# A range test of the softmax sums, and a general path behind a branch, in a fused attention and max-out kernel

## The chip, the core and the metric

The kernel runs on one core of a Trainium2 chip. The engines are TensorE (PE: matmul, with its weight loads shown apart as PEld), VectorE (DVE), ScalarE (ACT), GpSimd (POOL) and SyncE (SP), which here only issues DMA transfers. Each engine runs its own stream of instructions in order, and they wait for one another through semaphores. The metric is the device time of one execution in microseconds, lower is better.

## What is computed

Attention over queries that are averaged in pairs, followed by a two-branch max-out layer on the result:

```python
def _attn_ref(q, k, v):                       # q, k, v: (8, 8, 1152, 64)
    q_pool = q.reshape(B, H, S // 2, 2, D).mean(axis=3)
    scores = (1.0 / np.sqrt(D)) * np.matmul(q_pool, k.transpose(0, 1, 3, 2))
    scores = scores - np.max(scores, axis=-1, keepdims=True)
    attn = np.exp(scores)
    attn = attn / (np.sum(attn, axis=-1, keepdims=True) + 1e-09)
    return np.matmul(attn, v)
def _moe_ref(x, w1, w2, w_out):               # x: (4608, 512), d_ff 1024
    return np.maximum(x @ w1, x @ w2) @ w_out
```

The inputs q, k and v are normal draws times 0.1, so the scores are small.

## The kernel before

Work goes pair of heads by pair of heads, 32 pairs (8 batches of 4). For a pair, q, k and v are loaded by DMA (issued on SyncE), cast and pooled on GpSimd, and transposed (on PE at first, later k by a transposing DMA and q on DVE, L449). PE makes the scores in groups of 512 columns for both heads (L584), ACT takes their exponential into `et` (L591), and PE multiplies by v (L495, L507). v carries a column of ones, so the same product gives each row's sum of exponentials. **No row maximum is subtracted.** The exponential is taken of the raw scaled score, and the sum is inverted as it is.

The inversion and scaling are in `norm` (L513 to L529). A reciprocal on DVE (L517) goes into one of two small tiles `rc`, which are reused from pair to pair: 5 columns for the first head (4 chunks of 128 queries and one of 64 for both heads), 4 for the second. Products with it (L521, L525) go to `xnat`. `xnat` is transposed into `xT` (L633 by DMA, L646 on PE), and the max-out layer runs in between and after the last pair: L798/L771 (hidden layer), L807/L782/L778 (its ReLU of the difference), L831/L864 (output), L842/L891/L894/L876/L880 (copies out of PSUM), and the stores L745, L751 and L735. The last stores (L735) are issued half on SyncE, half on ScalarE.

Every instruction is recorded first (`Plan.op`) with the keys that it reads and writes. The order on PE, DVE, GpSimd and SyncE is then written out by hand, as one letter per instruction (`pe_order`, `dve_order`, `pool_order`, `sp_order`), and `Plan.solve` finds the semaphore waits. `Plan.emit` writes an engine's stream. Before, each stream stands in a block of its own (`nc.Block()`, L1449 to L1469). SyncE's stream ends with waits for the landings of all stores, and the block's end brings the five engines together in a barrier (L249).

Of the kernel before, what the change touches and what calls it, by code (L numbers as in the profile page):

```python
# [1 line left out]

# [2 lines left out]

FP32 = mybir.dt.float32
BF16 = mybir.dt.bfloat16
P = 128

EXP = mybir.ActivationFunctionType.Exp  # L10
RELU = mybir.ActivationFunctionType.Relu
COPY = mybir.ActivationFunctionType.Copy
ALU = mybir.AluOpType
AX = mybir.AxisListType


class Plan:
# [75 lines left out]
    def lane(self, o):  # L93
        key = (o["w"] or ("o",))[0]
        if o["eng"] == "PE":
            return "S" if key[0] == "s" else key[1:]
        if o["eng"] == "SP":
            return {"kT": "t"}.get(key[:2], key[0])
        if o["eng"] == "POOL":
            return {"kb": "k", "wd": "d"}.get(key[:2], key[0])  # L100
        for k in o["r"] + o["w"]:
            if k[0] == "f" and k[1:].isdigit():
                return k[1:]
        return {"qt": "T", "w2": "W", "wo": "W"}.get(key[:2], "Q")

    def reorder(self, want):

# [37 lines left out]
    def solve(self):  # L145
        ops = self.ops
        know = {}
        dma_seen = {}
        for n, o in enumerate(ops):
            eng = o["eng"]  # L150
            kn = know.setdefault(eng, {})
            o["waits"] = []
            for d in sorted(o["deps"], reverse=True):
                p = ops[d]
                if p["dma"] is None:
                    if p["eng"] == eng and not o["fence"] and (eng == "PE" or eng != "DVE" and d not in o["raw"]):
# [12 lines left out]
            if o["dma"] is not None:  # L169
                dma_seen[o["dma"]] = dma_seen.get(o["dma"], 0) + 1  # L170
                o["count"] = 16 * dma_seen[o["dma"]]
        need = set()
        for o in ops:
            need.update(o["waits"])
        cnt = {}
        for n, o in enumerate(ops):
            if o["dma"] is None:
                o["inc"] = n in need
# [34 lines left out]
        self.single = single  # L213


def bass_funnel_attn__then__act_maxout2_kernel(
    nc: bass.Bass,
    q: bass.AP,
# [19 lines left out]
    NC_ = C // P  # L238
    NF = F // P
# [3 lines left out]
    scale = 0.5 / float(D) ** 0.5  # L243
    W = 512
# [1 line left out]
    NGR = NPAIR * PW // W  # L246

    ctx = ExitStack()
    with ctx:  # L249
        def sbuf(shape, dt, name):  # L250
            return ctx.enter_context(nc.sbuf_tensor(name, list(shape), dt))

        def psum(shape, name):
            return ctx.enter_context(nc.psum_tensor(name, list(shape), FP32))

        ident = sbuf([P, P], BF16, "ident")
        qraw = [sbuf([P, QU, 2, D], FP32, f"qraw{s}") for s in range(3)]
# [36 lines left out]
        def rows(half):  # L294
            return slice(half * HP, half * HP + HP)
# [109 lines left out]
        def dve(fn, r, w, cost):  # L405
            op("DVE", fn, r=r, w=w, cost=cost)
# [73 lines left out]
        def av_jobs(i):  # L480
            b, h0 = i // NHP, 2 * (i % NHP)
            es = i % 2
            vs = i % 3
            xs = b % 2
            need = [f"et{es}.{g - first(i)}" for g in range(first(i), after(i))] + [f"vE{vs}", f"v.{i}"]

            def col(half, t, sb):
                return (half * 2 + es) * PW + flat(i, t, sb * P)

            def chunk(half, sb):  # L490

                def go(e, m):
                    for t in range(NT):
                        a = col(half, t, sb)
                        last = e.matmul(  # L495
                            fb[m][:, sb * 66:sb * 66 + 65], et[:, a:a + P],
                            vE[vs][:, t, half, 0:65], start=(t == 0), stop=(t == NT - 1))
                    return last
                return unit(need, 0.2755, go)

            def rest():

                def go(e, m):
                    for t in range(NT):
                        for half in range(2):
                            a = col(half, t, NCH)
                            last = e.matmul(  # L507
                                fb[m][rows(half), NCH * 66:NCH * 66 + 65], et[:, a:a + NB],
                                vE[vs][:, t, half, 0:65], start=(t == 0), stop=(t == NT - 1))
                    return last  # L510
                return unit(need, 0.308, go, "c")

            def norm(half):  # L513
                def evac(m):
                    n = NCH + 1 - half
                    a = fb[m][:, 0:(NCH + 1) * 66].rearrange("p (j c) -> p j c", c=66)
                    dve(lambda e: e.reciprocal(rc[half][:, 0:n], a[:, 0:n, 64:65]),  # L517
                        [f"f{m}"], [f"rc{half}"], 0.19)
                    if half == 0:
                        for k in range(2):  # L520
                            dve(lambda e, k=k: e.tensor_tensor(  # L521
                                xnat[xs][rows(0), i % NHP, NCH, k * D:k * D + D], a[rows(k), NCH, 0:D],
                                rc[0][rows(k), NCH:NCH + 1].to_broadcast([HP, D]), ALU.mult),
                                [f"f{m}", "rc0"], [f"xr{xs}.{h0 + k}"], 0.221)
                    dve(lambda e: e.tensor_tensor(  # L525
                        xnat[xs][:, i % NHP, 0:NCH, half * D:half * D + D], a[:, 0:NCH, 0:D],
                        rc[half][:, 0:NCH].unsqueeze(2).to_broadcast([P, NCH, D]), ALU.mult),
                        [f"f{m}", f"rc{half}"], [f"xn{xs}.{h0 + half}", f"f{m}"], 0.425)
# [847 lines left out]
        while p_end[0] < NTOK:  # L1376
# [81 lines left out]

        @block.vector
        def _(vc):  # L1460
            plan.emit("DVE", vc, sem)

        @block.scalar
        def _(ac):
            plan.emit("ACT", ac, sem)

        @block.tensor
        def _(pe):
            plan.emit("PE", pe, sem)  # L1469


# [26 lines left out]
```

## Time and profile before

| | us |
|---|---|
| median of 3 runs | 367.25 |
| lowest, highest | 365.64, 368.3 |
| span of the profiled execution | 368.9 |

The span is the time from the first to the last instruction of one profiled execution; it lies 1.65 above the median of the runs. In the listings, a line of a timeline has the start (us), the time taken, engine, source line, operation, output and input, and in square brackets the engine's idle time before it with what ended it. "SPq" and "ACTq" are the instructions of an engine's own sequencer, such as the issue of a transfer. A line of windows gives start and end, the length, then for PE, PEld, DVE, ACT and POOL the busy time with the number of instructions, the granted clock, the DMA share and GB/s. A line of a source line gives the number of its instructions, the shortest, median and longest in ns, and the first and last start in us. "To landing" is the time from the issue of a transfer to its arrival.

### The profile page before, as it was taken

The page shows a single profiled execution, that of the slowest core. Times are in us where ns is not written, and L with a number is a line of the kernel's source. Part 1 is how long each engine was busy: PE and PEld are TensorE (multiplying, and loading weights), DVE is VectorE, ACT ScalarE, POOL GpSimd, SP SyncE. Part 2 cuts the span into 40 slices and gives each one's busy share as a digit, 9 for nine tenths or more (in the row PEclk, how much of TensorE's full clock was granted, in tenths as well). Part 3 has the DMA queues.
Part 4 walks back from the last instruction along what each step waited for, and adds up shares of the span by engine and source line. Part 5 has one row for each costly group of instructions (what it writes and reads, how often), then busy time and mean ns, then how long its engine had stood idle before and what let it go on. Part 6 is the DMA issues. An engine that isn't in the chain of part 4 may idle for free.

```text
span 368.9 us, 13316 instructions
## 1 busy us (share of the span) xinstructions
PE 359.1 (97%) x5941; PEld 225.9 (61%) x5945; DVE 240.9 (65%) x521; ACT 315.6 (86%) x355; POOL 124.7 (34%) x111
## 2 busy tenths in 40 slices
PE   6999999999999999999999999999999999999996
PEld 5766564665556665657565665665666666556853
DVE  1478378867778867848885776577877766714411
ACT  4699989999999998999998999999999989895221
POOL 1256675533134333372242602525224440010000
PEclk9599999999999999999999999999999999999999
DMA  7999959999939998898999999998999680913206
GB/s 265 406 396 397 402 108 328 307 312 164 330 102 234 291 271 253 211 297 178 251 349 185 252 245 236 283 304 181 277 253 197 191 201 6 181 43 72 54 0 171
DMA packets 77640, 84.71 MB, mean 230 GB/s; under 512 B 49936, under 2 KB 50704, under 8 KB 77584
## 3 DMA queue, kind: packets, MB, share of 16 engines
q1 hardware_dynamic: 77024, 83.09, 84.8%
q8 instruction: 46, 0.75, 0.9%
q10 hardware_dynamic: 560, 0.79, 0.6%
q14 instruction: 10, 0.08, 0.1%
HBM read 62.91 MB, written 9.44 MB: 196 GB/s over the span
## 4 chain that ended last, share of the span: by engine, by line
PE 95%; DMA 2%; ACT 2%; issue 1%; SPq 0%; POOL 0%; DVE 0%; DVEq 0%
PE sps L584 22%; PE sps L495 12%; PE sps L831 11%; PE fb L831 10%; PE fb L495 9%; PE sps L798 8%; PE fb L798 7%; PE sps L864 3%; PE sps L507 2%; PE fb L716 2%; DMA kraw<-in_k_dram 2%; ACT et L591 2%; PE fb L507 1%; PE fb L864 1%; PE sps L771 1%; PE fb L319 1%
## 5 line engine op out<-in xcount | busy, mean ns | idle before, releaser
L591 ACT ACTIVATE et<-sps 128x1024 bf16<-128x1024 f32 (+1 forms) x336 | 307.6, 1002 | 25.1 <-PE sps L584 23.0
L584 PE MATMUL sps<-qpT,kT 64*128 64x256 bf16 (+7 forms) x1162 | 121.5, 287 | 1.0 <-issue 0.5
L449 DVE STREAM_TRANSPOSE qpT<-qp 32x288 bf16<-32x288 bf16 x216 | 101.3, 469 | 5.6 <-PE sps L584 1.5
L584 PEld LDWEIGHTS sps<-qpT,kT 64*128 64x128 bf16 x1162 | 49.6, 95 | 48.1 <-ACT et L591 15.8
L389 POOL TENSOR_TENSOR qp<-qraw 128x576 bf16<-128x576 f32 x30 | 42.1, 1406 | 98.2 <-DVE qpT L449 76.2
L395 POOL TENSOR_SCALAR vE<-vraw 128x1152 bf16<-128x1152 f32 x32 | 36.9, 1154 | 60.7 <-DMA vraw<-in_v_dram 60.7
L495 PE MATMUL sps<-vE,et 128*128 128x65 bf16 x1368 | 48.4, 193 | 0.0
L495 PEld LDWEIGHTS sps<-vE,et 128*128 128x128 bf16 x1368 | 43.6, 97 | 6.0 <-issue 5.3
L356 POOL TENSOR_SCALAR kbf<-kraw 128x1152 bf16<-128x1152 f32 x31 | 35.7, 1153 | 33.5 <-DMA kT<-kbf 16.5
L798 PE MATMUL sps<-xT,wd 64*128 64x512 bf16 (+3 forms) x368 | 43.7, 326 | 0.0
L831 PE MATMUL sps<-wo,stage 64*128 64x512 bf16 x256 | 36.8, 376 | 0.0
L495 PE MATMUL fb<-vE,et 128*128 128x65 bf16 x936 | 33.5, 193 | 0.5 <-issue 0.5
L798 PE MATMUL fb<-xT,wd 64*128 64x512 bf16 (+3 forms) x272 | 33.6, 333 | 0.1
L495 PEld LDWEIGHTS fb<-vE,et 128*128 128x128 bf16 x936 | 29.9, 97 | 5.5 <-issue 4.8
L831 PE MATMUL fb<-wo,stage 64*128 64x512 bf16 x224 | 33.0, 376 | 0.0
L807 DVE TENSOR_SCALAR stage<-sps 128x1024 bf16<-128x1024 f32 (+3 forms) x23 | 22.3, 969 | 15.7 <-PE sps L798 15.6
L798 PEld LDWEIGHTS sps<-xT,wd 64*128 64x128 bf16 x368 | 15.6, 94 | 13.7 <-PE sps L798 1.4
L807 DVE TENSOR_SCALAR stage<-fb 128x1024 bf16<-128x1024 f32 (+3 forms) x17 | 17.0, 999 | 10.7 <-PE fb L798 10.4
L517 DVE RECIPROCAL rc<-sps 128x5 f32<-128x5 f32 (+1 forms) x38 | 7.1, 186 | 19.7 <-PE sps L495 19.2
L831 PE MATMUL sps<-w,xT 64*128 64x512 bf16 x128 | 18.7, 377 | 0.0
L842 DVE COPY stage<-sps 128x1024 f32<-128x1024 f32 x8 | 9.8, 1225 | 12.8 <-PE sps L831 12.7
L831 PEld LDWEIGHTS sps<-wo,stage 64*128 64x128 bf16 x256 | 12.1, 94 | 9.5
(81 smaller groups left out, 296.6 us busy)
## 6 DMA issues: line engine op xcount, KB each, us to landing
vraw<-in_v_dram SPq DMA_DIRECT2D x32, 576.0 KB, 6.6
kraw<-in_k_dram SPq DMA_DIRECT2D x31, 576.0 KB, 6.6
qraw<-in_q_dram SPq DMA_DIRECT2D x31, 576.0 KB, 6.7
out_dram<-stage SPq DMA_DIRECT2D x21, 256.0 KB, 5.5
out_dram<-stage SPq DMA_DIRECT2D x23, 128.0 KB, 3.2
xT<-in_moe_w_dram SPq DMA_DIRECT2D x4, 512.0 KB, 10.7
stage<-in_moe_w_out_dram SPq DMA_DIRECT2D x4, 512.0 KB, 13.5
stage<-in_moe_w_dram SPq DMA_DIRECT2D x4, 512.0 KB, 13.1
```

Source lines behind the costliest of these rows:

```text
L356: op("POOL", lambda g: g.tensor_scalar(kbf[s][:, :, :, :].rearrange("p t h d -> p h t d"), kraw[r][:, :, :, :], 1.0, 1.0, ALU.mult, ALU.mu ...
L389: op("POOL", lambda g: g.tensor_tensor(qpf[s][:, :, :], qraw[r][:, :, 0, :], qraw[r][:, :, 1, :], ALU.add), r=[f"qraw{r}"], w=[f"qp{s}.0", ...
L395: op("POOL", lambda g: g.tensor_scalar(vE[r][:, :, :, 0:D].rearrange("p t h d -> p h t d"), vraw[r][:, :, :, :], 1.0, 1.0, ALU.mult, ALU.m ...
L449: op("DVE", lambda e: e.transpose(view[dst:dst + 32, :, 32 * pb:32 * pb + 32], qpf[s][src:src + 32, :, 32 * db:32 * db + 32]), r=[f"qp{s}. ...
L495: last = e.matmul(fb[m][:, sb * 66:sb * 66 + 65], et[:, a:a + P], vE[vs][:, t, half, 0:65], start=(t == 0), stop=(t == NT - 1))
L507: last = e.matmul(fb[m][rows(half), NCH * 66:NCH * 66 + 65], et[:, a:a + NB], vE[vs][:, t, half, 0:65], start=(t == 0), stop=(t == NT - 1))
L584: last = e.matmul(sps[r][:, h, col:col + hi - lo], kT[i % 3][rows(h), t, :], qpT[i % 3][rows(h), lo:hi], start=True, stop=True)
L591: op("ACT", lambda e: e.activation(et2[:, :, c:c + z - a], sps[r][:, :, a - g * W:z - g * W], EXP, scale=scale), r=[f"s{r}"], w=keys + ([f ...
L798: last = e.matmul(fb[m + k][:, 0:size], wd[z, ct, (f0 + k) * P:(f0 + k + 1) * P], xT[z, ct, n0:n1], start=(turn == 0 and ct == 0), stop=(t ...
L807: dve(lambda e: e.tensor_scalar_max(gT[:, f0:f0 + 2, g0:g0 + size], wide[m // 2][:, :, 0:size], 0.0), [f"f{m}", f"f{m + 1}"], w + [f"f{m}" ...
L831: last = e.matmul(fb[m + k][:, :], lhs, rhs, start=(turn == 0 and j == 0), stop=(turn == 1 and j == NC_ + NF - 1))
L864: return e.matmul(fb[m][:, 0:c1 - c0], lhs, rhs[:, c0:c1], start=(j == 0), stop=(j == NC_ + NF - 1))
```

## The change

All reciprocals are kept: `rc` becomes one tile `rcs` of 32 pairs by 9 columns. After the last pair DVE takes the largest and smallest of them, tests them against 1e18 and 1e-18, and SyncE turns the column of 128 results into a row by a DMA. DVE then takes the row's maximum into an integer `flag`. The five DVE instructions are put as "GGGGG" into `dve_order`, in front of the last three copies, and the DMA as "g" into `sp_order`, in front of the last seven stores.

The streams are no longer in blocks. At its end each engine waits for the flag, loads it into a register, and takes a branch: where the flag is not 0, a general path (`guarded`, about 120 lines) computes everything again in float32 with row maxima, in two loops over batches and over blocks of 128 tokens, and overwrites the output. Where it is 0, the engine goes on behind that path. There SyncE waits for the stores to land, and the engines meet in a barrier. With the inputs used here the flag is 0.

```diff
-        rc = [sbuf([P, NCH + 1], FP32, f"rc{s}") for s in range(2)]
+        rcs = sbuf([P, NPAIR, 2 * NCH + 1], FP32, "rcs")
...
-                    dve(lambda e: e.reciprocal(rc[half][:, 0:n], a[:, 0:n, 64:65]),
+                    dve(lambda e: e.reciprocal(rcs[:, i, half * (NCH + 1):half * (NCH + 1) + n], a[:, 0:n, 64]),
                         [f"f{m}"], [f"rc{half}"], 0.19)
...
+        allrc = rcs[:, :, :].rearrange("p i c -> p (i c)")
+        dve(lambda e: e.tensor_reduce(bad[:, 0:1], allrc, AX.X, ALU.max), ["rc0", "rc1"], ["gd0"], 0.4)
+        dve(lambda e: e.tensor_reduce(bad[:, 1:2], allrc, AX.X, ALU.min), ["rc0", "rc1"], ["gd1"], 0.4)
+        dve(lambda e: e.tensor_scalar(bad[:, 2:3], bad[:, 0:1], 1.0 / SUM_LO, 1.0, ALU.is_gt, ALU.mult),
+            ["gd0"], ["gd2"], 0.1)
+        dve(lambda e: e.scalar_tensor_tensor(bad[:, 3:4], bad[:, 1:2], 1.0 / SUM_HI, bad[:, 2:3],
+                                             ALU.is_lt, ALU.max), ["gd1", "gd2"], ["gd3"], 0.1)
+        op("SP", lambda e: e.dma_start(badr[0:1, :], bad[:, 3:4]), r=["gd3"], w=["gr"], dma="d_g")
+        dve(lambda e: e.tensor_reduce(flag[0:1, 0:1], badr[0:1, :], AX.X, ALU.max), ["gr"], ["gd4"], 0.2)
...
-            "TTT6666770T666667706666770302026025170026")
+            "TTT6666770T666667706666770302026025170GGGGG026")
...
-            "xqxxkvxktxootxxootxoovoooxoxxoxoooooooo")
+            "xqxxkvxktxootxxootxoovoooxoxxoxogooooooo")
...
-        block = ctx.enter_context(nc.Block())
-
-        @block.gpsimd
-        def _(g):
-            plan.emit("POOL", g, sem)
-
-        @block.sync
-        def _(sp):
-            plan.emit("SP", sp, sem, last_waits=[f"d_o{s}" for s in range(4)] + [f"d_z{s}" for s in range(4)])
...
+        taken = nc.alloc_registers("taken")
+        sure = [o["count"] for o in plan.ops if "gd4" in o["w"]][0]
+        for name, h in (("POOL", nc.gpsimd), ("SP", nc.sync), ("DVE", nc.vector), ("ACT", nc.scalar), ("PE", nc.tensor)):
+            plan.emit(name, h, sem)
+            h.wait_ge(sem["DVE"], sure)
+            h.reg_load(taken[h.engine], flag[0:1, 0:1])
+        room.close()
+        stored = [f"d_o{s}" for s in range(4)] + [f"d_z{s}" for s in range(4)]
+
+        def landed():
+            plan.emit("-", nc.sync, sem, last_waits=stored)
+
+        guarded(nc, taken, landed, q, k, v, moe_w1, moe_w2, moe_w_out, out)
+        landed()
+        nc.all_engine_barrier()
```

The general path begins with the branch:

```python
def guarded(nc, taken, landed, q, k, v, w1, w2, wo, out):
    ...
    with nc.If_ne(taken, 0):
        landed()
        nc.all_engine_barrier()
        with TileContext(nc) as tc:
            ...
```

More of the change, by code (lines that the diff above doesn't have):

```diff
@@ L4 @@
 from concourse import mybir
+from concourse.tile import TileContext
 FP32 = mybir.dt.float32
+I32 = mybir.dt.int32
 BF16 = mybir.dt.bfloat16
 P = 128
+SUM_LO, SUM_HI = 1.0 / 1e18, 1e18
 EXP = mybir.ActivationFunctionType.Exp
@@ L177, in solve @@
             if o["dma"] is None:
-                o["inc"] = n in need
+                o["inc"] = n in need or "gd4" in o["w"]
                 if o["inc"]:
@@ new lines, in softmax_head @@
+def softmax_head(nc, pool, ps, ident, q, k, v, out, b, h, scale):
+    B, H, S, D = q.shape
+    SQ, NT = S // 2, S // P
+    T3 = NT // 3
+    kf = pool.tile([P, NT, D], FP32, name="kf")
+    vf = pool.tile([P, NT, D], FP32, name="vf")
+    kT = pool.tile([D, NT, P], FP32, name="kTf")
+    nc.sync.dma_start(kf[:, :, :], k[bass.ds(b, 1), h, :, :].rearrange("b (p t) d -> (b p) t d", t=NT))
+    nc.sync.dma_start(vf[:, :, :], v[bass.ds(b, 1), h, :, :].rearrange("b (p t) d -> (b p) t d", t=NT))
+    for t in range(NT):
+        tp = ps.tile([P, P], FP32, name="tp")
+        nc.tensor.matmul(tp[0:D, :], kf[:, t, :], ident[:, :], start=True, stop=True)
+        nc.vector.tensor_copy(kT[:, t, :], tp[0:D, :])
+    for lo in range(0, SQ, P):
+        n = min(P, SQ - lo)
+        qf = pool.tile([P, 2, D], FP32, name="qf")
+        nc.sync.dma_start(
+            qf[0:n, :, :],
+            q[bass.ds(b, 1), h, 2 * lo:2 * lo + 2 * n, :].rearrange("b (p r) d -> (b p) r d", r=2))
+        qs = pool.tile([P, D], FP32, name="qs")
+        nc.vector.tensor_tensor(qs[0:n, :], qf[0:n, 0, :], qf[0:n, 1, :], ALU.add)
+        tq = ps.tile([P, P], FP32, name="tp")
+        nc.tensor.matmul(tq[0:D, 0:n], qs[0:n, :], ident[0:n, 0:n], start=True, stop=True)
+        qT = pool.tile([D, P], FP32, name="qTf")
+        nc.vector.tensor_copy(qT[:, 0:n], tq[0:D, 0:n])
+        sc = ps.tile([P, 3, 512], FP32, name="sc")
+        for c in range(3):
+            nc.tensor.matmul(sc[0:n, c, 0:T3 * P], qT[:, 0:n],
+                             kT[:, c * T3:c * T3 + T3, :].rearrange("d t p -> d (t p)"), start=True, stop=True)
+        top = pool.tile([P, 1], FP32, name="top")
+        nc.vector.tensor_reduce(top[0:n, :], sc[0:n, :, 0:T3 * P], AX.XY, ALU.max)
+        low = pool.tile([P, 1], FP32, name="low")
+        nc.vector.tensor_scalar(low[0:n, :], top[0:n, :], -scale, 1.0, ALU.mult, ALU.mult)
+        ex = pool.tile([P, 3, T3 * P], FP32, name="ex")
+        nc.scalar.activation(ex[0:n, :, :], sc[0:n, :, 0:T3 * P], EXP, bias=low[0:n, 0:1], scale=scale)
+        tot = pool.tile([P, 1], FP32, name="tot")
+        nc.vector.tensor_reduce(tot[0:n, :], ex[0:n, :, :], AX.XY, ALU.add)
+        den = pool.tile([P, 1], FP32, name="den")
+        nc.vector.tensor_scalar(den[0:n, :], tot[0:n, :], 1e-9, 1.0, ALU.add, ALU.mult)
+        inv = pool.tile([P, 1], FP32, name="inv")
+        nc.vector.reciprocal(inv[0:n, :], den[0:n, :])
+        eT = pool.tile([P, NT, P], FP32, name="eT")
+        for t in range(NT):
+            te = ps.tile([P, P], FP32, name="tp")
+            nc.tensor.matmul(te[:, 0:n], ex[0:n, t // T3, (t % T3) * P:(t % T3) * P + P], ident[0:n, 0:n],
+                             start=True, stop=True)
+            nc.vector.tensor_copy(eT[:, t, 0:n], te[:, 0:n])
+        av = ps.tile([P, D], FP32, name="av")
+        for t in range(NT):
+            nc.tensor.matmul(av[0:n, :], eT[:, t, 0:n], vf[:, t, :], start=(t == 0), stop=(t == NT - 1))
+        ao = pool.tile([P, D], FP32, name="ao")
+        nc.vector.tensor_tensor(ao[0:n, :], av[0:n, :], inv[0:n, 0:1].to_broadcast([n, D]), ALU.mult)
+        nc.sync.dma_start(out[bass.ds(b * SQ + lo, n), h * D:h * D + D], ao[0:n, :])
@@ new lines, in maxout @@
+def maxout(nc, pool, ps, ident, wt, out, n, NC_, NF):
+    w1, w2, wo = wt
+    x = pool.tile([P, NC_ * P], FP32, name="x")
+    nc.sync.dma_start(x[:, :], out[bass.ds(n * P, P), :])
+    xT = pool.tile([P, NC_, P], FP32, name="xTf")
+    for c in range(NC_):
+        tx = ps.tile([P, P], FP32, name="tx")
+        nc.tensor.matmul(tx[:, :], x[:, c * P:c * P + P], ident[:, :], start=True, stop=True)
+        nc.vector.tensor_copy(xT[:, c, :], tx[:, :])
+    g = pool.tile([P, NF, P], FP32, name="g")
+    for f in range(NF):
+        a = ps.tile([P, P], FP32, name="ha")
+        for c in range(NC_):
+            nc.tensor.matmul(a[:, :], w1[:, c, f * P:f * P + P], xT[:, c, :], start=(c == 0), stop=(c == NC_ - 1))
+        first = pool.tile([P, P], FP32, name="first")
+        nc.vector.tensor_copy(first[:, :], a[:, :])
+        z = ps.tile([P, P], FP32, name="hz")
+        for c in range(NC_):
+            nc.tensor.matmul(z[:, :], w2[:, c, f * P:f * P + P], xT[:, c, :], start=(c == 0), stop=(c == NC_ - 1))
+        nc.vector.tensor_tensor(g[:, f, :], z[:, :], first[:, :], ALU.max)
+    y = ps.tile([P, NC_ * P], FP32, name="y")
+    for f in range(NF):
+        nc.tensor.matmul(y[:, :], g[:, f, :], wo[:, f, :], start=(f == 0), stop=(f == NF - 1))
+    o = pool.tile([P, NC_ * P], FP32, name="o")
+    nc.vector.tensor_copy(o[:, :], y[:, :])
+    nc.sync.dma_start(out[bass.ds(n * P, P), :], o[:, :])
@@ L248, in bass_funnel_attn__then__act_maxout2_kernel @@
     ctx = ExitStack()
-    with ctx:
+    outer = ExitStack()
+    outer.enter_context(ctx)
+    room = ExitStack()
+    bad = outer.enter_context(nc.sbuf_tensor("bad", [P, 4], FP32))
+    badr = outer.enter_context(nc.sbuf_tensor("badr", [1, P], FP32))
+    flag = outer.enter_context(nc.sbuf_tensor("flag", [1, 1], I32))
+    with outer:
         def sbuf(shape, dt, name):
-            return ctx.enter_context(nc.sbuf_tensor(name, list(shape), dt))
+            return room.enter_context(nc.sbuf_tensor(name, list(shape), dt))
         def psum(shape, name):
-            return ctx.enter_context(nc.psum_tensor(name, list(shape), FP32))
+            return room.enter_context(nc.psum_tensor(name, list(shape), FP32))
         ident = sbuf([P, P], BF16, "ident")
@@ L526, in evac @@
                         xnat[xs][:, i % NHP, 0:NCH, half * D:half * D + D], a[:, 0:NCH, 0:D],
[L527 removed]
+                        rcs[:, i, half * (NCH + 1):half * (NCH + 1) + NCH].unsqueeze(2).to_broadcast([P, NCH, D]), ALU.mult),
                         [f"f{m}", f"rc{half}"], [f"xn{xs}.{h0 + half}", f"f{m}"], 0.425)
```

44 lines of the change are left out of this document (33 added, 11 removed).

## The prediction

> **What bounds the kernel now.** I read the page first (span, busy shares, chain of waits), then the last 30 us by windows and timeline, then the single lines behind the end.
>
> ```profile
> span 368.9 us, 13316 instructions
> ...
> PE 359.1 (97%) x5941; PEld 225.9 (61%) x5945; DVE 240.9 (65%) x521; ACT 315.6 (86%) x355; POOL 124.7 (34%) x111
> ...
> PE 95%; DMA 2%; ACT 2%; issue 1%; SPq 0%; POOL 0%; DVE 0%; DVEq 0%
> ```
>
> TensorE is busy for 97% of the span and is 95% of the chain. Work on another engine costs nothing unless it delays a matmul or stands behind the last one. So the question is what the change puts where: does the test fit into DVE's idle time, and what stands after the last matmul? Windows of the last stretch:
>
> ```profile
> 352.05:359.50 7.45, 7.45 (x38) 3.46 (x36) 0.00 (x1) 1.70 (x5) 0.00 (x0) 1.00 0.00 0
> 359.50:366.40 6.90, 5.73 (x37) 3.10 (x36) 1.67 (x3) 1.65 (x3) 0.00 (x0) 1.00 0.68 190
> 366.40:368.90 2.50, 0.00 (x0) 0.00 (x0) 0.00 (x0) 0.00 (x0) 0.00 (x0) 0.75 0.38 105
> ```
>
> The columns after the length are PE, PEld, DVE, ACT and POOL busy, the granted clock, the DMA share and GB/s. From 352.05 to 359.50 PE is full, DVE does nothing and no DMA moves. In the last 2.50 us no engine computes; only stores are under way. The same stretch on DVE, SyncE's queue and ScalarE's queue:
>
> ```profile
> 351.63 0.42 DVE L782 TENSOR_SCALAR stage<-fb 128x256 bf16<-128x256 f32 x1
> 359.51 0.69 DVE L894 COPY stage<-fb 128x512 f32<-128x512 f32 x1 [7.46 <-PE fb L864]
> ...
> 365.42 0.29 DVE L880 COPY stage<-sps 128x128 f32<-128x128 f32 x1 [2.67 <-PE sps L864]
> ```
> ```profile
> 341.24 0.63 SPq L745 DMA_DIRECT2D out_dram<-stage  x1
> 358.94 7.45 SPq L735 DMA_DIRECT2D out_dram<-stage  x7
> ```
> ```profile
> 365.29 1.39 ACTq L735 DMA_DIRECT2D out_dram<-stage  x2
> ```
>
> SyncE issues its last store until 358.94 + 7.45 = 366.39, ScalarE until 366.68. How the kernel ends, from the lines of the waits and of the block's end:
>
> ```profile
> L735 SPq DMA_DIRECT2D out_dram<-stage x7: 466/467/595, 358.9 to 365.8; - x7
> ...
> DMA to landing us min/median/max: 2.2/2.4/3.0
> ```
> ```profile
> L204 SPq EVENT_SEMAPHORE  x4: 17/28/28, 368.2 to 368.4; - x4
> ```
> ```profile
> L249 PEldq DRAIN  x1: 1835/1835/1835, 363.5 to 363.5; - x1
> L249 DVEq DRAIN  x1: 305/305/305, 365.5 to 365.5; - x1
> L249 ACTq DRAIN  x1: 397/397/397, 366.7 to 366.7; - x1
> L249 SPq COMPARE_BRANCH  x1: 41/41/41, 368.5 to 368.5; - x1
> L249 SPq DRAIN  x1: 7/7/7, 368.7 to 368.7; - x1
> ```
>
> SyncE stands from 366.39 to 368.2 at the first wait for a store: 1.8 us of cover for anything put there. Then come four waits (368.2 to 368.4 in three steps, 0.07 each), a jump out of the block (368.5 to the drain at 368.7, 0.2) and the barrier (368.7 to 368.9, 0.2).
>
> **The change, part by part.** *The test on DVE.* It stands between L782 at 351.63 and L894 at 359.51. It has two reductions of 128x288 f32 (32 pairs of 9 reciprocals), two operations on 128x1, and after a DMA a reduction of 1x128.
>
> ```profile
> L673 DVE TENSOR_REDUCE wo<-stage 128x1024 bf16<-128x1024 f32 x4 | 4.8, 1212 | 0.0
> ...
> L517 DVE RECIPROCAL rc<-sps 128x5 f32<-128x5 f32 x19 | 3.7, 195 | 18.2 <-PE sps L495 18.0
> ```
>
> A 128x1024 reduction takes 1.21, so 288 columns lie between 0.34 (by columns) and 0.47 (L782's 0.42 for 256, scaled up); I take 0.47. The small operations are nearest to the 195 ns reciprocal: 0.2 each. The first four are done at 352.05 + 2 x 0.47 + 2 x 0.2 = 353.4. SyncE's queue is free from 341.87 to 358.94, so its 512 B transfer goes at once. It lands 2.2 to 3.0 us later by the stores' landings, with no other DMA moving: 356.4 at most. With 0.2 for the last reduction the flag stands at 356.6, 2.9 before L894 is wanted. Behind that wait on DVE stand only the last three copies, and behind the wait of the small transfer on SyncE only the seven stores from 358.94. I cost it at 0. If the transfer took over 6 us, L894 and the stores behind it would slip by the excess.
>
> *The reciprocals* go into one tile that keeps all of them; shapes, counts and order stay (5 and 4 columns). 0, as DVE is idle a third of the span.
>
> *The start.* The jumps into the five blocks go. No line of the trace stands for them, so nothing is saved. SyncE gains four register moves ahead of its first barrier.
>
> ```profile
> L1483 SPq DRAIN  x1: 7/7/7, 0.0 to 0.0; - x1
> ...
> L1483 POOLq MOVE  x1: 35/35/35, 0.1 to 0.1; - x1
> ...
> L1483 POOLq EVENT_SEMAPHORE  x2: 17/17/17, 0.6 to 0.7; - x2
> ```
>
> At 35 ns they are 0.14, and GpSimd closes this barrier at 0.6, so 0; uncovered they would cost that 0.14.
>
> *The end.* After its last instruction every engine waits for the flag (there since 356.6: 0.02 by the waits of 17 to 28 ns), loads it into a register, compares and jumps over the general path. In the built program the jump passes about 460 instructions on SyncE, 890 on DVE, 4,170 on TensorE, 140 on ScalarE and 70 on GpSimd. On SyncE this stands behind its last store at 366.39 and ahead of the waits for the stores. Three costs follow.
>
> The load L: the trace has none. Low end 0.07, a step of one wait; high end 2.2, a transfer to memory and back. I take 0.5: it reads one word and has no descriptor and no DMA engine in it, so it is nearer the low end. [...]
>
> The jump B: 0.2, as the step from COMPARE_BRANCH to the drain.
>
> The code behind the jump, F. Code comes in by its own transfers:
>
> ```profile
> q8 instruction: 46, 0.75, 0.9%
> ...
> q14 instruction: 10, 0.08, 0.1%
> ```
>
> q8 carries 0.75 MB / 46 = 16 KB a time and, with 46 transfers for 11,900 TensorE instructions, is TensorE's: 256 instructions each. q14 carries 0.08 MB / 10 = 8 KB, which at the same 64 B is 128 instructions, for the other engines. A jump of 460 instructions on SyncE passes over three such pieces, 4,170 on TensorE over sixteen, 140 on ScalarE about one. The jump of before (COMPARE_BRANCH) goes to the next instructions and shows no stall. F is 0 if the target is there already, and a transfer asked for and waited for if not: 2.4 by the median landing, 3.0 by the slowest; two in a row, 6.0. I take 2.4. [...]
>
> The sum on SyncE: 366.39 + 0.02 + 0.5 + 0.2 + 2.4 = 369.5. By then the stores landed long ago (368.2), so the four waits pass at 4 x 0.07 = 0.28, and the barrier takes 0.2: 369.99. The old end was 368.9, so +1.1. The others are no later: TensorE drains from 363.5 and DVE from 365.5, so with the same 3.1 they arrive at 366.6 and 368.6 (half a microsecond more for TensorE's larger piece changes nothing); ScalarE at 366.7 + 3.1 = 369.8 even if it must fetch, level with SyncE; GpSimd has been waiting all along.
>
> The profiled execution, 368.9, is 1.65 above the median of the three runs (367.25) and 0.6 above the highest. The work at the end does not scale, so I carry +1.1 over: 367.25 + 1.1 = **368.4**.
>
> **The rivals.** With X = L + B + F, the end is 366.39 + 0.02 + X + 0.48 where X is over 1.8.
>
> *Covered.* X stays under 1.8: the target is there already, or a small fetch is much quicker than a store. Then the stores' landing at 368.2 still sets the end, and the jump out of the block (0.2) is gone: 367.25 - 0.2 = 367.1. For it: q14's transfers are 8 KB alone, their share small. Against it: 460 instructions are more than three of them.
>
> *Slower by over 1%: two fetches in a row on SyncE's path.* If the piece with the target is followed by a second that the last instructions need, each at the slowest landing, F is 6.0 and X = 6.7: 366.41 + 6.7 + 0.48 = 373.6, +4.7, so 372.0. It decides from X = 5.7 on (+3.7). For it: nothing else runs ahead of that code, and three engines ask within some 2 us of each other, amid the last stores. Against it: only some ten instructions stand behind the target.
>
> *The test overruns its gap.* The slowest landings in the trace are
>
> ```profile
> stage<-in_moe_w_out_dram SPq DMA_DIRECT2D x4, 512.0 KB, 13.5
> ```
>
> At 13.5 the flag would stand at 353.4 + 13.5 + 0.2 = 367.1 and L894 would slip 7.6: 374.9. Those moved 512 KB among many others; here nothing else moves.
>
> *The change doesn't do what it says*, that is, the branch is not hidden by the stores: that is my forecast itself, with 1.8 of 3.1 covered.
>
> **How the numbers follow.** Forecast (X between 1.8 and 5.7, so 367.1 to 370.9): 0.55. Covered, 367.1: 0.25. Two fetches, 372.0: 0.15. Overrun, 374.9: 0.02. Something that I don't see makes it faster by over 1%: 0.03. One per cent, 3.7 us, is about what a measurement of this kernel tells from no change: its three runs lie 2.7 apart. Faster by over 1%: the 0.03, and 0.01 of scatter in the covered case, 0.04. Slower by over 1%: 0.15 + 0.02 = 0.17. Within 1%: the rest of forecast and covered, 0.79. The range goes from 366.5 (covered, 0.6 of scatter) to 371.5 (X = 5.7 and 0.6), and leaves out the two slow cases and the fast one, 0.2 in all.
>
> **What would show it.** In the profile of the changed kernel the test's five DVE lines lie between 352 and 357 and L894 still starts as soon as PE has finished its bank. SyncE's last store is followed by a register load of some 0.5 us and a branch, then by 2 to 3 us without an instruction, and q14 moves one or two more pieces after 365. The waits for the stores pass at once, and the span's last window without compute is 3.6 rather than 2.5 long. I'm wrong if SyncE reaches its waits before the stores land, if ScalarE or TensorE arrives last, or if a stretch before 352 has moved.

## The result and the profile after

| | us |
|---|---|
| before, median of 20 runs (lowest, highest) | 367.13 (365.54, 369.56) |
| after, median of 20 runs (lowest, highest) | 368.71 (366.84, 370.71) |
| ratio after / before, 95% interval | 1.0043 (1.0024 to 1.0062) |
| profiled execution of after, time and span | 368.65, 366.9 |

The change costs 0.0043 x 367.13 = 1.6 us (0.9 to 2.3). That is within 1%, and its interval doesn't hold zero. The page of after, its first lines and the two queues that bring code:

```profile
span 366.9 us, 13339 instructions
...
PE 355.2 (97%) x5945; PEld 222.7 (61%) x5945; DVE 242.2 (66%) x526; ACT 315.0 (86%) x355; POOL 124.6 (34%) x111
...
q8 instruction: 48, 0.79, 0.9%
...
q14 instruction: 15, 0.12, 0.1%
```

TensorE is as full as it was (97%), and the code queues moved two more pieces of 16 KB (q8) and five more of 8 KB (q14). But the span is 2.0 *shorter* than the 368.9 of before, while the runs say that the kernel is slower. (A run's time is some 1.7 longer than its span, as 368.65 and 366.9 here. So a span can't be set beside a median of times: by that 1.7 the profiled execution of before lay some 3.4 above its median, an estimate, and not the 1.65 that is given with the time before and in the prediction.) Before any stage is compared, one must see why. The first 18 us by windows, before and then after (length, PE, PEld, DVE, ACT, POOL, granted clock, DMA share, GB/s):

```profile
0.00:9.20 9.20, 6.35 (x71) 5.48 (x72) 1.73 (x6) 3.94 (x5) 1.61 (x10) 1.00 0.76 266
9.20:18.40 9.20, 8.78 (x97) 6.70 (x95) 3.84 (x7) 6.33 (x7) 2.31 (x2) 0.50 1.03 405
```
```profile
0.00:9.20 9.20, 7.45 (x91) 6.13 (x91) 2.28 (x8) 4.46 (x6) 1.60 (x10) 1.00 0.76 250
9.20:18.40 9.20, 8.29 (x156) 6.20 (x157) 6.55 (x9) 9.20 (x11) 2.30 (x2) 1.00 1.03 403
```

The profiled execution of before had a bad start: the granted clock was 0.50 in the second window, and 71 + 97 = 168 matmuls were done by 18.4 where the other had done 91 + 156 = 247. The change touches nothing there. So the two spans can't be set against each other, and I compare from a mark near the end. I call the *tail* the time from the start of the last copy on DVE to the end of the span. Before it is 368.88 - 365.42 = 3.46. (From the start of the last matmul, which some expectations below use, it is 0.35 longer: 3.82 before, 5.86 after.)

The end of after on DVE, on SyncE's queue, and the stretch without compute:

```profile
347.65 0.42 DVE L912 TENSOR_SCALAR stage<-fb 128x256 bf16<-128x256 f32 x1
347.99 0.44 DVE L1544 TENSOR_REDUCE bad<-rcs 128x1 f32<-128x288 f32 x1
348.35 0.44 DVE L1545 TENSOR_REDUCE bad<-rcs 128x1 f32<-128x288 f32 x1
348.71 0.14 DVE L1546 TENSOR_SCALAR bad<-bad 128x1 f32<-128x1 f32 x1
348.89 0.16 DVE L1548 SCALAR_TENSOR_TENSOR bad<-bad 128x1 f32<-128x1 f32 x1
351.04 0.27 DVE L1551 TENSOR_REDUCE flag<-badr 1x1 int32<-1x128 f32 x1 [2.00 <-DMA badr<-bad]
355.54 0.69 DVE L1024 COPY stage<-fb 128x512 f32<-128x512 f32 x1 [4.22 <-PE fb L994]
...
361.44 0.29 DVE L1010 COPY stage<-sps 128x128 f32<-128x128 f32 x1 [2.67 <-PE sps L994]
```
```profile
349.08 0.54 SPq L1550 DMA_DIRECT2D badr<-bad  x1
354.97 7.89 SPq L865 DMA_DIRECT2D out_dram<-stage  x7
```
```profile
362.90:366.42 3.52, 0.00 (x0) 0.00 (x0) 0.00 (x0) 0.00 (x0) 0.00 (x0) 0.69 0.24 64
```

The flag stands at 351.04 + 0.27 = 351.31, and the next copy (L1024, which was L894) starts 4.22 later, still released by PE. So the test costs nothing. The tail is 366.94 - 361.44 = **5.50**, 2.04 more than before. It is in the end. SyncE's stores take from 354.97 to 362.86, 7.89 where they took 7.45. The lines of the stores, the register loads, the branches and the barrier (count, then shortest/median/longest in ns, first and last start):

```profile
L865 SPq DMA_DIRECT2D out_dram<-stage x7: 466/467/1037, 355.0 to 361.8; - x7
L865 ACTq DMA_DIRECT2D out_dram<-stage x7: 497/498/1007, 355.0 to 361.9; - x7
```
```profile
L1594 POOLq TENSOR_LOAD <-flag x1: 487/487/487, 351.4 to 351.4; - x1
L1594 PEldq TENSOR_LOAD <-flag x1: 613/613/613, 359.5 to 359.5; - x1
...
L1594 ACTq TENSOR_LOAD <-flag x1: 986/986/986, 362.9 to 362.9; - x1
L1594 SPq TENSOR_LOAD <-flag x1: 803/803/803, 362.9 to 362.9; - x1
```
```profile
L207 SPq EVENT_SEMAPHORE  x4: 28/28/28, 366.4 to 366.6; - x4
L207 POOLq COMPARE_BRANCH  x1: 45/45/45, 351.9 to 351.9; - x1
L207 PEldq COMPARE_BRANCH  x1: 3712/3712/3712, 360.2 to 360.2; - x1
L207 DVEq COMPARE_BRANCH  x1: 72/72/72, 362.1 to 362.1; - x1
L207 SPq COMPARE_BRANCH  x1: 58/58/58, 363.8 to 363.8; - x1
L207 ACTq COMPARE_BRANCH  x1: 54/54/54, 363.9 to 363.9; - x1
```
```profile
L1603 PEldq DRAIN  x1: 73/73/73, 364.0 to 364.0; - x1
L1603 ACTq DRAIN  x1: 79/79/79, 364.4 to 364.4; - x1
L1603 DVEq DRAIN  x1: 57/57/57, 365.1 to 365.1; - x1
L1603 SPq DRAIN  x1: 13/13/13, 366.7 to 366.7; - x1
```

Read down SyncE. Its last store ends at 362.86, the load takes 0.80 from 362.9, the branch stands at 363.8, and then nothing until the first of the four waits at 366.4: 2.6 without an instruction. The barrier needs SyncE last, as the others drain from 364.0, 364.4 and 365.1. Against before:

| on SyncE | before | after |
|---|---|---|
| start of the last copy to end of the last store's issue | 0.97 | 1.42 |
| from there to the first wait | 1.81 | 3.56 |
| from there to the end | 0.68 | 0.52 |
| tail | 3.46 | 5.50 |

The first row is a surprise: the longest store issue on SyncE went from 595 to 1037 ns, on ScalarE's queue from 847 to 1007. The second row is SyncE's own: by the records of the landings the last store was there at 365.00, and SyncE passes its first wait only at 366.42. Before, these two lie 0.02 apart (368.19 and 368.21).

### The profile page after: what moved, and what is told of

Its sections match the earlier page's. It is cut to its first block, busy times and chain, and to the rows that moved or that the text cites. A ratio compares the mean times of both kernels' runs of the same rounds, so it can differ in the third digit from the quotient of the medians.

```text
span 366.9 us, 13339 instructions
## 1 busy us (share of the span) xinstructions
PE 355.2 (97%) x5945; PEld 222.7 (61%) x5945; DVE 242.2 (66%) x526; ACT 315.0 (86%) x355; POOL 124.6 (34%) x111
## 4 chain that ended last, share of the span: by engine, by line
PE 92%; ACT 4%; DMA 1%; issue 1%; SPq 0%; POOL 0%; DVE 0%; DVEq 0%
PE sps L714 20%; PE sps L625 12%; PE sps L961 11%; PE fb L961 10%; PE fb L625 9%; PE sps L928 9%; PE fb L928 7%; ACT et L721 4%; PE sps L994 3%; PE sps L637 2%; PE fb L846 2%; PE fb L637 2%; PE fb L994 1%; PE sps L901 1%; DMA kraw<-in_k_dram 1%; PE fb L901 1%
## 5 line engine op out<-in xcount | busy, mean ns | idle before, releaser
L714 PE MATMUL sps<-qpT,kT 64*128 64x256 bf16 (+7 forms) x1162 | 118.3, 283 | 0.3 <-DVE kT L601 0.2
L714 PEld LDWEIGHTS sps<-qpT,kT 64*128 64x128 bf16 x1162 | 48.0, 94 | 47.5 <-ACT et L721 15.5
L647 DVE RECIPROCAL rcs<-sps 128x5 f32<-128x5 f32 (+1 forms) x38 | 7.0, 184 | 19.8 <-PE sps L625 19.3
```

The source lines that it names most:

```text
L714: last = e.matmul(sps[r][:, h, col:col + hi - lo], kT[i % 3][rows(h), t, :], qpT[i % 3][rows(h), lo:hi], start=True, stop=True)
```

## The experiments

The first theory was the prediction's: the load, the jump and the code behind it on SyncE are all of the cost, and the test and the missing blocks are nothing. The rivals: the longer stream before the end costs something (tried by the test alone and by the kernel before without its block); the load alone does it (the loads without the branch); the distance of the jump doesn't matter (the near jump). When the longer store issue was seen, a second question came up: who holds it? All ratios are to the kernel before on the same chip in the same batch of runs.

**The test without load, branch and path.**

```diff
-            h.wait_ge(sem["DVE"], sure)
-            h.reg_load(taken[h.engine], flag[0:1, 0:1])
...
-        guarded(nc, taken, landed, q, k, v, moe_w1, moe_w2, moe_w_out, out)
```

> The test of the sums stays (five DVE instructions, the small transfer, the tile of all reciprocals) and the streams stay without blocks; the register load, the branch and the general path are left out. Theory (the cost is all on SyncE between its last store and its waits: load 0.8 us, jump, 2.6 us of waiting for code): equal to the kernel before, 367.0 us, or 0.2 less, and SyncE stands at its first wait for a store from the issue of its last store on. Rival (the test itself, its transfer or the moved buffers cost): 368.6 us, as with the whole change.

Ratio 0.9989 (0.9956 to 1.0023). The tail is 3.24, 0.22 under before, and the store issues are back:

```profile
L865 SPq DMA_DIRECT2D out_dram<-stage x7: 467/467/595, 354.7 to 361.5; - x7
L865 ACTq DMA_DIRECT2D out_dram<-stage x7: 497/499/836, 354.7 to 361.5; - x7
```

The test, its DMA and the reciprocals cost nothing that can be measured: the times leave room for 0.8 us, the tail for none. So the cost comes with the load, the branch and the path.

**The kernel before without its block** (the five streams emitted straight, then the waits and a barrier, no test):

```diff
-        block = ctx.enter_context(nc.Block())
...
+        for name, h in (("POOL", nc.gpsimd), ("SP", nc.sync), ("DVE", nc.vector), ("ACT", nc.scalar), ("PE", nc.tensor)):
+            plan.emit(name, h, sem)
+        plan.emit("-", nc.sync, sem, last_waits=[f"d_o{s}" for s in range(4)] + [f"d_z{s}" for s in range(4)])
+        nc.all_engine_barrier()
```

> The kernel before with its streams emitted straight, without the block, and nothing of the test: what that part does alone. Theory (the jump out of the block goes from SyncE's end): 0.2 us less than the kernel before, below what the times tell apart; in the profile the end from the last matmul's start is 3.6 instead of 3.8 us. Rival (the blocks cost or save something elsewhere in the stream): a difference over 1 us.

Ratio 1.0005 (0.9977 to 1.0033), tail 3.26. The jump out of the block is the 0.20 that the tail lost, here and in the run above; the times can't resolve it.

**The loads without the branch** (only the call of `guarded` dropped).

> As the first, and every engine waits for the flag and loads it into a register; the branch and the general path are left out. Theory: the load takes about 0.8 us on SyncE and lies within the 1.8 us for which it waits for its last store anyway, so 367.0 us, equal to the kernel before. Rival (the load is what costs): 0.8 to 1.5 us more, 367.9 to 368.6.

Ratio 0.9985 (0.9957 to 1.0013), tail 3.23. This run told nothing of the load: with no branch to use the registers, the built program holds no load at all, only the waits for the flag.

**A near jump.** The two loops of the general path are left out of it, so that each engine's jump passes 4 to 8 instructions; flag, loads and branches stay.

```diff
     with nc.If_ne(taken, 0):
         landed()
         nc.all_engine_barrier()
-        with TileContext(nc) as tc:
-            ...
-        with TileContext(nc) as tc:
-            ...
```

> Test, load and branch stay; of the general path only its first waits and its barrier stay, the two loops are left out, so each engine's jump passes 4 to 8 instructions instead of 72 to 4,173. Theory (a far target has to be fetched): load 0.8, jump 0.1 to 0.5 as on ScalarE in the changed kernel, together under 1.8, so 367.0 us, equal to the kernel before. Rival (a taken branch costs, near or far): about 368.6, with 2.6 us between the branch and the first wait on SyncE.

Ratio 0.9993 (0.9965 to 1.0022), but the profile's tail was 4.47, 1.01 over before. The two disagreed, so it ran again in a later batch.

> The near jump again (the two loops of the general path left out). The first profile showed an end of 4.8 us, 1.0 more than before, while the times showed no difference (ratio 0.9993, 0.9965 to 1.0022). If TensorE's code transfer always falls into the last two stores, the profile shows 4.8 again and the ratio is near 1.0027; if it does so only now and then, the profile shows 3.6 to 4.8 and the ratio stays near 1.0.

Ratio 1.0021 (0.9993 to 1.0049), tail 4.39. The second run fits its tail (+0.77 us by the ratio, +0.93 by the tail); the first lies a little under it. A near jump thus costs at most 0.0049 x 366.64 = 1.8 us, and by the profile some 0.9 to 1.0. The 2.6 us stall is gone, but the store issues are still long. Stores, then loads and branches, then the q8 row of the stretch 359.4 to 361.9:

```profile
L837 SPq DMA_DIRECT2D out_dram<-stage x7: 466/467/1246, 354.2 to 361.0; - x7
L837 ACTq DMA_DIRECT2D out_dram<-stage x7: 497/499/1215, 354.2 to 361.1; - x7
```
```profile
L207 SPq EVENT_SEMAPHORE  x4: 28/28/28, 364.5 to 364.7; - x4
...
L207 PEldq COMPARE_BRANCH  x1: 344/344/344, 359.4 to 359.4; - x1
...
L207 SPq COMPARE_BRANCH  x1: 58/58/58, 363.2 to 363.2; - x1
```
```profile
q8 instruction: 1, 0.02, 3.5%
```

TensorE passes its near jump in 344 ns, and a 16 KB piece comes on q8 all the same. In the records of the single transfers it begins 1.1 after the branch and lasts 1.41. SyncE's and ScalarE's last issues both end 0.33 after it. That named a suspect: TensorE's code transfer holds the stores.

**The near jump without TensorE.** As the near jump, and TensorE neither loads nor branches. The barrier inside the path, which all five engines would have to enter, is left out too. In the built program only SyncE then has a load and a branch, since the others have nothing left to jump over. So this takes away more than TensorE's part.

```diff
     with nc.If_ne(taken, 0):
         landed()
-        nc.all_engine_barrier()
...
-            h.wait_ge(sem["DVE"], sure)
-            h.reg_load(taken[h.engine], flag[0:1, 0:1])
+            if name != "PE":
+                h.wait_ge(sem["DVE"], sure)
+                h.reg_load(taken[h.engine], flag[0:1, 0:1])
```

> As the near jump (the two loops of the general path left out), and TensorE neither loads the flag nor branches; the other four do. In the near-jump run the last stores were issued in 1.33 and 1.30 us instead of 0.60 and 0.84, and they landed 1.2 us later, beside a code transfer of TensorE's queue that its branch started. Theory (that code transfer holds the last stores up): without TensorE's branch the last two issues take 0.60 and 0.84 us again, no code transfer falls into the last stores, and the end is 3.6 us from the start of the last matmul. Rival (the register loads of DVE, ScalarE and SyncE hold them up): 1.3 us again, and an end of 4.8 us.

Ratio 0.9990 (0.9962 to 1.0019), tail 3.24.

```profile
L836 SPq DMA_DIRECT2D out_dram<-stage x7: 467/467/597, 354.1 to 361.0; - x7
L836 ACTq DMA_DIRECT2D out_dram<-stage x7: 498/499/838, 354.1 to 361.0; - x7
```
```profile
L207 SPq EVENT_SEMAPHORE  x4: 28/28/28, 363.3 to 363.5; - x4
L207 SPq COMPARE_BRANCH  x1: 58/58/58, 362.5 to 362.5; - x1
```

No q8 transfer in this stretch, and issues of 597 and 838 ns. SyncE's load (836 ns) and near branch are done 0.7 ahead of the first wait at 363.3: the stores' landing covers them whole. This is the forecast's cover at work: in this run load and near jump cost nothing on SyncE, and from 359 on no code transfer stands in the trace.

What holding does to the landing shows in ScalarE's last store of 32 KB. From its issue to its arrival (the last number) it took 3.4 us in the second near-jump run, and 2.3 without TensorE:

```profile
out_dram<-stage ACTq DMA_DIRECT2D x1, 32.0 KB, 3.4
```
```profile
out_dram<-stage ACTq DMA_DIRECT2D x1, 32.0 KB, 2.3
```

By the records of the landings the last store of the near-jump run was there at 364.49, and SyncE's first wait passed at 364.50. So SyncE's near jump was covered in that run too: the late landing alone made its tail longer. Each of these stores reports its landing in sixteen parts. In the changed kernel, for the last six stores, the last part comes 0.16 to 1.10 behind the fifteenth (0.87 and more in four of them); in the kernel before it is at most 0.06. What keeps the last part back isn't shown.

**SyncE branches early.** The whole change, with SyncE's load and branch put right behind the small transfer; its last seven stores stand behind the branch, on both of its sides.

```diff
-    def emit(self, eng, h, sem, last_waits=()):
+    def emit(self, eng, h, sem, last_waits=(), part=None):
...
+        early = {"SP": nc.sync}
...
-            plan.emit(name, h, sem)
+            plan.emit(name, h, sem, part=0 if name in early else None)
...
         def landed():
+            for name, h in early.items():
+                plan.emit(name, h, sem, part=1)
```

> The whole change, but SyncE loads the flag and takes its branch right behind the small transfer, ahead of its last seven stores, which then stand on both sides of the branch. Theory: SyncE's load and fetch, some 3.4 us, fall into its idle time before the first of those stores; the end is set by the landing of the last store again, or by DVE, which comes back from its own branch 0.1 us later than that: 367.0 to 367.4 us, 1.3 to 1.6 less than the whole change. Rival (the cost is not SyncE's jump): stays near 368.6.

Ratio 1.0024 (1.0000 to 1.0049), tail 4.49. It was run again beside the whole change:

> SyncE's branch ahead of its last stores again, against the whole change on the same chip. Theory: 0.7 to 1.0 us less than the whole change (SyncE's gap gone, the slower last store on ScalarE still there), end 4.8 us from the last matmul's start, ratio to the kernel before 1.002 to 1.003.

> The changed kernel again, on one chip with the next two. From the profile of the first time the end, from the start of the last matmul, was 5.9 us against 3.8 before: 1.3 more for SyncE's wait for code (beyond the 1.8 us of cover) and some 0.4 for the slower issue of its last store, the rest in the load. Theory: the same again, 5.7 to 6.2 us, ratio 1.004 to 1.006, and the last issues end 0.4 us after TensorE's code transfer. Rival (the slower issue was chance): the last issue takes 0.60 us and the end is 5.4.

The whole change: 1.0056 (1.0029 to 1.0083), tail 5.81. SyncE early: 1.0020 (0.9995 to 1.0044), tail 4.09. The medians are 368.92 and 367.42, 1.5 apart on one chip (0.9 to 2.2, by resampling the twelve runs of each). SyncE's load and branch of the second run, and its waits:

```profile
L1597 SPq TENSOR_LOAD <-flag x1: 477/477/477, 350.4 to 350.4; - x1
```
```profile
L209 SPq EVENT_SEMAPHORE  x4: 28/28/28, 364.0 to 364.2; - x4
```

The load stands at 350.4, 3.6 ahead of the first of the last seven stores at 354.0, and nothing stands between the last store and the waits. What is left over before (0.63 of tail) is the store issue, 1087 ns on SyncE here, and with it the landing, at 364.03, just ahead of the first wait. In the first run SyncE's last issue was through in 597 ns, but ScalarE's took 1461. So SyncE's stall is the larger part of the cost, shown by removing it, and the held store is the rest. On SyncE alone there is little more to gain: DVE, back from its own far jump, drains at 364.27, level with SyncE's last wait.

**The far jump as the last instruction.** The whole change, but with flag 0 an engine goes on into its waits and the barrier, and only then jumps over the path.

```diff
-    with nc.If_ne(taken, 0):
+    with nc.body("path"):
...
+        for h in engs:
+            h.br_ne(taken[h.engine], 0, on_true="path", on_false="short")
+        with nc.body("short"):
+            landed()
+            nc.all_engine_barrier()
+            nc.br("after_path")
```

> The whole change in another layout: where the flag is 0 an engine falls through to the waits for the stores and the barrier, which stand right behind the branch, and jumps over the general path only behind that barrier, as its last instruction. Theory (the far jump between the last store and the waits is the cost): the waits are reached about 1 us after the last store, under the cover of the landing; 367.0 us if the far jumps behind the barrier lie outside the time, up to 370 if the execution is counted until they are done. TensorE takes no jump before the barrier, so the last stores are issued in 0.60 and 0.84 us. Rival (a compare with a register costs in itself): the barrier is no earlier than in the changed kernel, 5.9 us from the last matmul's start.

Ratio 1.0104 (1.0067 to 1.0141), tail 7.08: the worst of all. The stores, TensorE's two branches:

```profile
L867 SPq DMA_DIRECT2D out_dram<-stage x7: 466/468/595, 355.5 to 362.3; - x7
L867 ACTq DMA_DIRECT2D out_dram<-stage x7: 497/498/836, 355.5 to 362.4; - x7
```
```profile
L1605 PEldq COMPARE_BRANCH  x1: 90/90/90, 360.7 to 360.7; - x1
```
```profile
L1609 SPq COMPARE_BRANCH  x1: 38/38/38, 365.2 to 365.2; - x1
...
L1609 PEldq COMPARE_BRANCH  x1: 3785/3785/3785, 365.2 to 365.2; - x1
```

Up to the barrier at 365.2 it goes as fast as before, 3.2 after the last copy (361.93). All five engines load the flag and compare, and the store issues are short: 595 and 836. So neither loads nor compares that fall through hold the stores. In every run with a jump of TensorE that is taken ahead of the end, they are held. But TensorE's far jump of 3.8 us now stands behind the barrier, uncovered, and it counts: nothing waits for it, yet the execution ends with it.

**Hints ahead of the branches.** The whole change, with a mark for the branch 40 instructions ahead of the end on TensorE (at 351.4, its branch at 360.6), and behind the small transfer and the flag on SyncE and DVE, meant to bring the target's code early.

```diff
+            if n == at:
+                hints[h.engine] = h.mark_branch_hint_location()
...
+        b = h.br_ne(taken[h.engine], 0, on_true="path", on_false="after_path")
+        if h.engine in hints:
+            b.branch_hint(hints[h.engine])
```

> The whole change, and ahead of the branch TensorE (some 8 us), DVE and SyncE (behind the flag and behind the small transfer) each get a hint instruction that names the branch and its target. Theory (the cost is the waiting for the target's code): the code comes in beforehand, SyncE's gap of 2.6 us between branch and first wait falls to about 0.3 and TensorE's and DVE's likewise; 367.0 to 367.4 us, the end 3.6 to 4.3 us from the last matmul's start instead of 5.9. Rival (the jump itself costs, wherever its code lies): 368.7 and 5.9 us.

Ratio 1.0093 (1.0062 to 1.0124), tail 6.01.

```profile
L230 PEldq COMPARE_BRANCH  x1: 3793/3793/3793, 360.6 to 360.6; - x1
...
L230 SPq COMPARE_BRANCH  x1: 78/78/78, 364.2 to 364.2; - x1
```
```profile
L212 SPq EVENT_SEMAPHORE  x4: 27/28/28, 367.1 to 367.3; - x4
```

TensorE's branch still takes 3.8 and SyncE still stands from 364.2 to 367.1. The hints shortened neither; why isn't known. Whether they cost something isn't either, as this interval overlaps that of the whole change.

Time and tail of all runs together (the difference by the ratio, times the median before of the batch; tail in us):

| kernel | tail over before | time over before, us (95%) | longest issue SyncE / ScalarE, ns |
|---|---|---|---|
| test alone | -0.22 | -0.4 (-1.6 to 0.8) | 595 / 836 |
| without block | -0.20 | 0.2 (-0.8 to 1.2) | 595 / 836 |
| loads without branch (no load in the built program) | -0.23 | -0.5 (-1.6 to 0.5) | 594 / 835 |
| near jump, no TensorE | -0.22 | -0.4 (-1.4 to 0.7) | 597 / 838 |
| near jump, first run | 1.01 | -0.3 (-1.3 to 0.8) | 1328 / 1300 |
| near jump, second run | 0.93 | 0.8 (-0.3 to 1.8) | 1246 / 1215 |
| SyncE early, first run | 1.03 | 0.9 (0.0 to 1.8) | 597 / 1461 |
| SyncE early, second run | 0.63 | 0.7 (-0.2 to 1.6) | 1087 / 1058 |
| the change (the 20 runs above) | 2.04 | 1.6 (0.9 to 2.3) | 1037 / 1007 |
| the change, second time | 2.35 | 2.1 (1.1 to 3.0) | 885 / 855 |
| with hints | 2.55 | 3.4 (2.3 to 4.5) | 1271 / 1241 |
| far jump last | 3.62 | 3.8 (2.5 to 5.2) | 595 / 836 |

The tail of one profile lies inside the interval of the time in all rows but the first run of the near jump, where it lies just outside.

## Why the prediction was right, and where its terms were off

The forecast, 368.4 with a cost of 1.1, was right in its sign, and in its place and mechanism on SyncE; the runs give 368.71 and 1.6 (0.9 to 2.3), and the tail 2.04. By its steps:

- *The test in DVE's gap*: right, with room. The reductions took 0.44 for the estimated 0.47, the small operations 0.14 and 0.16 for 0.2, the transfer's result came 1.96 after its issue began (349.08 to 351.04) where up to 3.0 was allowed. The spare is 4.2 for the forecast 2.9. The run with the test alone confirms it (0.9989).
- *The reciprocals and the start*: 0, as forecast; the same run holds both.
- *The load L*: 0.5 was taken, and SyncE's took 0.80: 0.3 too little. On the other engines it took 0.49 (GpSimd) to 0.99 (ScalarE). The nearer end of the bounds was rightly chosen, and the row for it was missing. That no DMA engine has a part in it shows on GpSimd: around its load, from 351.3 to 351.9, the trace of the changed kernel has no DMA packet.
- *The jump and the code behind it, B + F*: 2.6 was taken, and 2.65 passed on SyncE from the start of the branch to the first wait. Taking the median landing of a store as the price of a code fetch was lucky rather than reasoned. In the records of single transfers of the changed kernel, DVE's branch ends at 362.21, an 8 KB transfer (the only one between 353 and 364.7) begins 1.07 later and lasts 0.42, and the drain follows 1.41 behind it. On TensorE the 16 KB transfer begins 1.04 after the branch does and lasts 1.25, and the branch ends 1.42 behind it. Between SyncE's branch and its first wait three 8 KB transfers begin (364.73, 365.02 and 365.70), of 0.44 to 0.49. The records of q14 don't name an engine, so SyncE's own split is not shown.
- *ScalarE, reckoned with a fetch as level with SyncE*, didn't wait for one. From the start of its branch to its drain it takes 0.48, GpSimd 0.45; their targets are 140 and 70 instructions away. DVE, at 890, drains 2.97 after its branch begins; SyncE, at 460, comes to its first wait after 2.65; TensorE's branch, at 4,170, takes 3.71. So the two short jumps went without a stall and the three long ones with one. From which distance on a jump stalls isn't shown. Nor need a code transfer be a stall. In the second near-jump run TensorE's branch takes 344 ns and the drain behind it is over by 360.6, while the 16 KB transfer, begun 1.1 after the branch, lasts until 361.9. In the changed kernel one 8 KB transfer begins 1.02 after GpSimd's branch, at 352.94, and GpSimd had gone on by 352.3.
- *The cover of 1.8*: right, and 2.14 in the changed kernel, as the stores landed later (362.86 to 365.00). The near jump without TensorE shows load and branch vanish under the landing of the stores.
- *The last stores*: the forecast left their issue as it was. This is the term that it missed: the issue on SyncE ended 0.45 later. By the sum on SyncE: 0.45 of held issue, plus X (load, jump and code, with the wait for the flag) = 3.56 where 3.12 was reckoned, less 0.16 for the jump out of the block where 0.2 was. The tail's 2.04 is so 0.93 over the 1.1 of the forecast, half from the held stores and half from X, two thirds of that the load.

Of the rivals, the covered end would be the near jump on SyncE alone; with the whole path it didn't come. Two fetches in a row on SyncE's path would have made X 6.7, and it was 3.56.

What stays open: whether anything beside TensorE's taken jump takes part in holding the stores, as the run without it lacked three other branches too. Two of these can be left out: in the near-jump runs GpSimd's comes ten microseconds earlier, and ScalarE's stands behind its own last store. DVE's taken jump (361.3, amid the last issues) remains as a rival. Open are also how a transfer of TensorE's code holds an issue on SyncE and ScalarE, and the first near-jump time. No version with the whole path beat the kernel before; SyncE early is the cheapest of them, and its interval touches no change.

## What to carry to other kernels

A runtime branch at the end of this kernel cost what its *taken* side made the last engine wait for: 0.5 to 1.0 us for the register, and 2.65 (SyncE, over 460 instructions) to 3.8 us (TensorE, over 4,170) for a far jump, during which code transfers ran. In these runs it was free only on an engine that branched while something longer was still under way, so put the branch of the engine that closes the kernel ahead of its last waits and stores, not behind them; that took the cost from 2.1 to 0.7 us here. And when two spans disagree with the runs, look for a difference that the change can't have made, and compare from a mark behind it.

## What the runs showed of the hardware that was not expected

- In every run with a taken jump on TensorE before the end, near or far, a 16 KB code transfer begins 1.0 to 1.2 after the branch does (1.8 in the first run with SyncE early), and the issue of the last store on SyncE, ScalarE or both ends about 0.3 to 0.4 after that transfer does. On SyncE it takes 885 to 1328 ns instead of 595 (597 in the first run with SyncE early), on ScalarE 855 to 1461 instead of 836. In the whole change the transfer ran from 361.24 to 362.48, and both issues ended at 362.86. Where no such transfer falls there, the issues are short, in every run. That the transfer is the cause is argued from this and from the run without TensorE's jump, with the rival named above.
- A jump that is the last instruction of an engine, behind the barrier, is still part of the measured time: 3.8 us for TensorE.
- The load of one word into a register takes 0.48 to 0.99 us, and on SyncE 0.48 early in a quiet stretch (350.4) against 0.73 to 0.84 among the last stores.
